# A recurrence and its FFN on one core: a new order for all jobs, and four chunks loaded in runs of 2 KB

## Chip, cores, metric

The kernel runs on one core of a Trainium2 chip. The metric is the device time of one execution, in microseconds (us), the median of several runs. TensorE is called PE here, VectorE DVE, ScalarE ACT, GpSimd POOL, SyncE SP.

## What is computed

A gated linear recurrence along 5824 time steps (4 sequences, 256 channels), then a multiplicative FFN without an activation on all 23296 tokens. Cut to what matters:

```python
a_base = 1.0 / (1.0 + np.exp(-a_param))
log_a = 8.0 * sig_r * np.log(np.clip(a_base, 1e-06, 1.0 - 1e-06))[None, None, :]
a_t = np.exp(log_a)
x_gated = np.sqrt(np.maximum(1.0 - a_t * a_t, 1e-06)) * sig_i * x
for t in range(S):
    h = a_t[:, t] * h + x_gated[:, t]
    y[:, t] = h
...
a = y @ w1
b = y @ w2
out = (a * b @ w3) @ w_out
```

`sig_r` and `sig_i` are the sigmoids of `r_gate` and `i_gate`; w1 and w2 are 256 x 1024, w3 is 1024 x 1024, w_out 1024 x 256.

## The kernel before

The tokens are cut into 47 chunks: chunks 0 and 1 and the last (46) have 256 tokens, the others 512. w3 and w_out are multiplied once at the start (the "fold", `Ft`, `Fc`, `Fm`, `Fe`, eight parts), so that each chunk needs two up projections and one down projection. All products are in bf16.

One chunk passes through these jobs, each a word of the order, with the chunk's number behind it:

- `r`, `i`, `x` (`load`, line 151): three DMAs on SP, 512 KB each. Partition p gets row p of each of four blocks of 128 tokens, in runs of 1 KB. Chunks 0, 2, 3, 4 and 7, which PE turns ("long rows"), have four tokens in a row on a partition instead.
- `R`, `I` (lines 160 to 168): tanh on ACT. `p`, `t` (173, 189, 192): u = (tanh + 1) x, mostly on POOL, the second in two halves.
- `V`, `U` (lines 200, 211): the tanh of r and u are turned, so that channels lie on partitions: by PE into PSUM for a few early chunks, by a transposing DMA on SP for the others (tiles `rt` and `ut`).
- `d` (`decay`, 223): a = exp on ACT, for each half of the channels. `s` (`square`, 231, 233): a squared, on ACT, DVE or POOL, by tables. `q` (`root`, 238): sqrt(1 - a a) on ACT, behind a table load, since exp and tanh share a table that sqrt is not in.
- `g` (`gated`, 248, 251): max and product with the turned u, on DVE, in place. `h` (`scan`, 270): the recurrence, on DVE, two scans a chunk. `y` (`cast`, 280, 282): to bf16, mostly on POOL.
- `a`, `b` (`up`, 299): the up projections on PE in four pairs of 128 columns of w1 and w2; `a` comes in two halves of two matmuls, each with its own PSUM tile, `b` has four matmuls into one PSUM pair. `c` (`copy`, 320 on DVE, 322 on ACT): a half of `a` from PSUM to bf16. `m` (`product`, 337): a times b on DVE, from PSUM.
- `D` (`down`, 357): eight matmuls for 128 tokens. `e` (`evac`, 320, 322): two such results from PSUM. `o` (`store`, 380): to memory, on SP.

`W` (`warm`, 287) are pairs of matmuls on a constant, whose results nobody reads. `L` and `C` load and cast weights.

Every tile comes from a ring of a few buffers (`ring`): among others four PSUM tiles "po" for `a`, `D` and turns, and two PSUM pairs "pb" for `b` and `W`. A tile is taken again when the last reader of its former holder is done, so a matmul can wait for a copy four tiles back, and a `b` for the product of two before. The order of the work is written out by hand in the string `ORDER`, 2449 words, each issued on its engine as it comes; each engine runs its own instructions strictly in that order. Which engine takes a movable job is set by tables ahead of it (`DV_COPY`, `DV_EVAC`, `AC_SQUARE`, `DV_HALF`, `AC_CAST` and others): a copy listed in `DV_COPY`, say, goes to DVE, any other to ACT.

Of the kernel before, what the change touches and what calls it, by code (L numbers as in the profile page):

```python
# [664 lines left out]
```

## Time and profile before

| | |
|---|---|
| time, median of 3 runs | 511.43 us (511.33 to 511.6) |
| span of the profiled execution, first to last instruction | 509.1 us |
| what lies around the span (median less span) | 2.3 us |
| PE busy | 501.7 us, 99%, 3225 matmuls |
| ACT busy | 461.5 us, 91% |
| DVE busy | 431.8 us, 85% |
| POOL busy | 318.0 us, 62% |
| DMA packets on the 16 engines | 85% of the span, 124 MB |

The page gives no time of its own for the profiled execution beside its span. Shares are means over the span: the first 26 us, in which weights arrive, and the last 60, in which the recurrence is over, differ from the middle. "Busy" of PE counts overlapping matmuls, so that it says that PE had work, and not at what rate; durations of single matmuls contain the tail behind the last column.

### The profile page before, as it was taken

The page shows a single profiled execution, that of the slowest core. Times are in us where ns is not written, and L with a number is a line of the kernel's source. Part 1 is how long each engine was busy: PE and PEld are TensorE (multiplying, and loading weights), DVE is VectorE, ACT ScalarE, POOL GpSimd, SP SyncE. Part 2 cuts the span into 40 slices and gives each one's busy share as a digit, 9 for nine tenths or more (in the row PEclk, how much of TensorE's full clock was granted, in tenths as well). Part 3 has the DMA queues.
Part 4 walks back from the last instruction along what each step waited for, and adds up shares of the span by engine and source line. Part 5 has one row for each costly group of instructions (what it writes and reads, how often), then busy time and mean ns, then how long its engine had stood idle before and what let it go on. Part 6 is the DMA issues. An engine that isn't in the chain of part 4 may idle for free.

```text
span 509.1 us, 8891 instructions
## 1 busy us (share of the span) xinstructions
PE 501.7 (99%) x3225; PEld 308.3 (61%) x3225; DVE 431.8 (85%) x417; ACT 461.5 (91%) x708; POOL 318.0 (62%) x269
## 2 busy tenths in 40 slices
PE   7999999999999999999999999999999999999997
PEld 3767665665665656556656556565566655656566
...
GB/s 317 410 411 345 335 316 282 305 286 259 310 220 298 279 285 247 211 302 196 247 305 327 254 286 148 252 243 227 210 246 164 235 298 161 85 166 62 65 51 104
DMA packets 178048, 124.06 MB, mean 244 GB/s; under 512 B 87378, under 2 KB 174036, under 8 KB 178004
## 3 DMA queue, kind: packets, MB, share of 16 engines
...
q8 instruction: 25, 0.41, 0.4%
...
## 4 chain that ended last, share of the span: by engine, by line
PE 92%; ACT 3%; DMA 2%; POOL 1%; DVE 1%; issue 1%; SPq 1%; ACTq 0%; DVEq 0%
PE po L357 30%; PE pb L299 29%; PE pa L299 29%; DMA wf<-in_moe_w_dram 2%; PE pw L436 1%; ACT sa L322 1%; PE ptr L200 1%; PE ptw L425 1%; POOL u_t L192 0%; DVE h_t L270 0%; SPq L151 0%; ACT ot L322 0%; SPq L407 0%; ACT L168 0%; ACT L238 0%
## 5 line engine op out<-in xcount | busy, mean ns | idle before, releaser
L337 DVE TENSOR_TENSOR g_t<-sa,pb 128x1024 bf16<-128x1024 bf16 (+1 forms) x188 | 218.7, 1180 | 58.9 <-PE pb L299 27.6
L299 PEld LDWEIGHTS <-w_sb 128*128 128x128 bf16 x1504 | 146.4, 98 | 144.1 <-issue 1.4
L322 ACT CAST sa<-pa 128x512 bf16<-128x512 f32 (+1 forms) x332 | 179.8, 591 | 27.1 <-PE pa L299 18.9
L299 PE MATMUL pa<-y_t,w_sb 128*128 128x512 bf16 (+1 forms) x752 | 190.2, 372 | 0.2 <-ACT sa L322 0.2
L299 PE MATMUL pb<-y_t,w_sb 128*128 128x512 bf16 (+1 forms) x752 | 184.9, 372 | 0.2 <-ACT w_sb L414 0.2
L357 PE MATMUL po<-wp_sb,g_t 128*128 128x256 bf16 (+1 forms) x1464 | 177.6, 272 | 0.0
L357 PEld LDWEIGHTS <-g_t 128*128 128x128 bf16 x1464 | 142.5, 98 | 39.5 <-issue 0.3
L282 POOL CAST y_t<-h_t 128x1024 bf16<-128x1024 f32 (+2 forms) x47 | 53.8, 1145 | 140.2 <-DVE h_t L270 136.1
L192 POOL TENSOR_TENSOR u_t<-i_t,x_t 128x512 bf16<-128x512 f32 (+1 forms) x90 | 123.3, 1387 | 3.8 <-DMA ut<-u_t 1.8
L270 DVE TENSOR_TENSOR_SCAN h_t<-a_t,h_t,nrm 128x512 f32<-128x512 f32 (+1 forms) x92 | 121.1, 1343 | 1.6
L233 POOL TENSOR_TENSOR nrm<-a_t 128x512 f32<-128x512 f32 x70 | 78.4, 1137 | 7.0 <-ACT a_t L223 4.0
L223 ACT ACTIVATE a_t<-rt,la 128x512 f32<-128x512 bf16 (+1 forms) x82 | 66.1, 823 | 0.0
L322 ACT COPY ot<-po 128x512 f32<-128x512 f32 x84 | 49.1, 589 | 13.2 <-PE po L357 12.9
L173 POOL TENSOR_SCALAR i_t<-i_t 128x1024 f32<-128x1024 f32 (+1 forms) x45 | 55.4, 1233 | 8.3 <-ACT i_t L168 8.3
L251 DVE SCALAR_TENSOR_TENSOR nrm<-nrm,ut 128x1024 f32<-128x1024 f32 (+1 forms) x39 | 53.2, 1365 | 5.2 <-ACT nrm L238 5.2
L168 ACT ACTIVATE i_t<-i_t 128x1024 f32<-128x1024 f32 (+1 forms) x46 | 48.5, 1063 | 0.3 <-DMA i_t<-in_i_gate_dram 0.2
L238 ACT ACTIVATE nrm<-nrm 128x1024 f32<-128x1024 f32 (+1 forms) x47 | 48.4, 1040 | 0.2
L162 ACT ACTIVATE th_r<-r_t 128x1024 bf16<-128x1024 f32 (+1 forms) x41 | 43.5, 1064 | 0.0
L320 DVE CAST sa<-pa 128x512 bf16<-128x512 f32 x36 | 23.5, 684 | 1.4 <-PE pa L299 0.8
L238 ACT ACT_TABLE_LOAD x17 | 21.8, 1283 | 0.4
L287 PE MATMUL warm<-ident 128*128 128x512 bf16 x32 | 10.7, 473 | 1.6 <-DVE ident L441 1.6
L231 ACT ACTIVATE nrm<-a_t 128x512 f32<-128x512 f32 x18 | 11.4, 645 | 0.0
...
## 6 DMA issues: line engine op xcount, KB each, us to landing
...
rt<-th_r SPq DMA_TRANSPOSE x41, 4.7
ut<-u_t SPq DMA_TRANSPOSE x39, 4.4
```

What stands on the lines that cost most here:

```text
L173: (nc.vector if c in DV_PLUS else nc.gpsimd).tensor_scalar(t, t, 1.0, 1.0, op0=ALU.add, op1=ALU.mult)
L192: (nc.vector if (c, half) in DV_HALF else nc.gpsimd).tensor_mul(out=u, in0=t, in1=xt)
L223: nc.scalar.activation(out=a, in_=pr, func=AF.Exp, scale=la4[:, cb:cb + 1], bias=la4[:, cb:cb + 1])
L233: (nc.vector if (c, cb) in DV_SQUARE else nc.gpsimd).tensor_mul(out=n, in0=a, in1=a)
L238: nc.scalar.activation(out=n, in_=n, func=AF.Sqrt, scale=-1.0, bias=1.0)
L251: nc.vector.scalar_tensor_tensor(out=n, in0=n, scalar=1e-3, in1=T["pu", c][:, :, cols], op0=ALU.max, op1=ALU.mult)
L270: nc.vector.tensor_tensor_scan(h[:, cb, :], a[:, cb, :], n[:, cb, :], init, ALU.mult, ALU.add)
L282: (nc.vector if key in DV_CAST else nc.gpsimd).tensor_copy(out=y, in_=h)
L299: nc.tensor.matmul(out=dst, lhsT=w_sb[:, cb, m * P:(m + 1) * P], rhs=T["y", gates_of(c)][:, cb, span(c, mp)], start=(cb == 0), stop=(cb == ...
L322: nc.scalar.copy(out=dst, in_=src_ps)
L337: nc.vector.tensor_mul(out=T["g", z][:, 2 * mp:2 * mp + 2, span(c, mp)], in0=T["sa", c, mp][:, :, :w], in1=T["pb", c, mp][:, :, :w])
L357: nc.tensor.matmul(out=po, lhsT=T["g", c][:, k, j * P:(j + 1) * P], rhs=wp_sb[:, k, cols], start=(k == 0), stop=(k == KD - 1), skip_group_ ...
```

## The change

All 2449 words are the same; up to word 1500 (chunk 27's first up matmul is word 1503) they stand in another order, and the remaining 949 are as before, word for word. The tables have new entries for chunks 0 to 32 where they ended at chunk 16. In all, 34 copies `c` and 4 output copies `e` go from ACT to DVE, 11 squares from POOL to ACT, three halves of u from POOL to DVE, two casts `y` from POOL to ACT; single weight casts and fold steps change engines. PE has the same instructions, and no more and no fewer warm matmuls.

Chunks 38 to 41 are loaded so that a partition gets two tokens in a row (2 KB), twice. Their turned tiles hold the tokens in another order, and decay and gating put them right: in chunks 38 and 39 they read the turned tile in steps of 128 elements, in 40 and 41 they read in a row and write every other float. Gating takes four instructions of 256 elements a chunk instead of one of 1024.

```diff
-    DV_HALF = set()
...
+    DV_HALF = {(9, 1), (16, 0), (30, 1)}
...
+    AC_CAST = {22, 24}
...
+    FOLD_ACT = {('c', 7), ('e', 6), ('e', 7)}
...
+    PAIR_IN = {38, 39}
+    PAIR_OUT = {40, 41}
...
+    def in_pairs(c):
+        return c in PAIR_IN or c in PAIR_OUT
+
+    def split_in(t):
+        return t.rearrange("p (h q j) -> p h q j", h=2, q=P)
+
+    def split_turned(t):
+        return t.rearrange("p (h j q) -> p h j q", h=2, q=P)
...
+        if in_pairs(c):
+            rows = src[nm][starts[c]:starts[c] + width(c), :].rearrange("(h p n) c -> p h n c", h=2, p=P)
+            nc.sync.dma_start(out=T[nm, c].rearrange("p (h n) c -> p h n c", h=2), in_=rows)
+            return
         nc.sync.dma_start(out=T[nm, c][:, :n, cols], in_=rows[:, :, cols])
...
         if long_rows(c):
             a, pr = in_time(a, w // P), turned(pr)
+        elif c in PAIR_IN:
+            a, pr = split_in(a), split_turned(pr).rearrange("p h j q -> p h q j")
+        elif c in PAIR_OUT:
+            a, pr = split_in(a).rearrange("p h q j -> p h j q"), split_turned(pr)
         nc.scalar.activation(out=a, in_=pr, func=AF.Exp, scale=la4[:, cb:cb + 1], bias=la4[:, cb:cb + 1])
...
+        if in_pairs(c):
+            for cb in range(NCB):
+                for hh in range(2):
+                    half = slice(hh * 2 * P, (hh + 1) * 2 * P)
+                    n, u = in_time(T["n", c][:, cb, half], 2), turned(T["pu", c][:, cb, half])
+                    if c in PAIR_OUT:
+                        n, u = n.rearrange("p q j -> p j q"), u.rearrange("p q j -> p j q")
+                    nc.vector.scalar_tensor_tensor(out=n, in0=n, scalar=1e-3, in1=u, op0=ALU.max, op1=ALU.mult)
             return
         n = T["n", c][:, :, cols]
...
-        r0 i0 x0 Lw1.1 Lw1.0 r2 i2 Lw2.0 Lw3.2 x2 E W13 A3. A0. A1. A2. R0.1 R0.0 W3 W10 V0.0 V0.1 I0 t0.1 d0.0 s0.0
-        d0.1 s0.1 q0.0 t0.0 Cw1.1 q0.1 Cw1.0 R2 I2 W5 W8 W0 U0 W4 W11 W6 W12 W7 W9 W2 g0 h0.1 h0.0 y0.1 y0.0 a0.0.1
...
+        r0 E W0 A3. A0. A1. A2. W11 W1 R0.1 V0.1 W7 i0 R0.0 V0.0 I0 x0 W3 t0.0 d0.1 Lw1.1 d0.0 Lw1.0 W4 W15 t0.1
+        Cw1.1 W14 U0 Cw1.0 r2 W12 s0.0 s0.1 q0.0 g0 W10 h0.1 h0.0 W2 i2 Lw2.0 q0.1 W5 g1 W6 y0.1 x2 h1.1 h1.0
...
```

The order at three places. First ACT, from the cast of the first half of w2 to the tanh of chunks 3 and 4. In the order before, `y_t` is chunk 1's, `a_t_249` and `nrm_262` are chunk 2's, `sa` are copies of products of chunks 0 and 1, `r_t_257` and `r_t_364` chunks 3 and 4:

```order
L414 CAST w2_sb_91<-wf_111 128x2x512
L280 CAST y_t_217<-h_t_214 128x256
L223 ACTIVATE a_t_249<-ptr_230,la4_85 128x512 x2
L231 ACTIVATE nrm_262<-a_t_249 128x512 x2
L238 ACT_TABLE_LOAD
L238 ACTIVATE nrm_262<-nrm_262 128x1024
L322 CAST sa_358<-pa_301 128x2x256
L160 ACT_TABLE_LOAD
L160 ACTIVATE th_r_390<-r_t_257 128x1024
L322 CAST sa_399<-pa_350 128x2x256
L322 CAST sa_401<-pa_339 128x2x256
L160 ACTIVATE th_r_431<-r_t_364 128x1024
```

In the new order (`a_t_280` and `nrm_283` are chunk 2's, `r_t_266` and `r_t_270` chunks 3 and 4):

```order
L447 CAST w2_sb_91<-wf_201 128x2x512
L247 ACTIVATE a_t_280<-ptr_228,la4_85 128x512 x2
L255 ACTIVATE nrm_283<-a_t_280 128x512 x2
L262 ACT_TABLE_LOAD
L262 ACTIVATE nrm_283<-nrm_283 128x1024
L355 CAST sa_342<-pa_326 128x2x256
L355 CAST sa_362<-pa_346 128x2x256
L355 CAST sa_369<-pa_364 128x2x256
L180 ACT_TABLE_LOAD
L180 ACTIVATE th_r_379<-r_t_266 128x1024
L180 ACTIVATE th_r_382<-r_t_270 128x1024
L247 ACTIVATE a_t_426<-ptr_416,la4_85 128x512 x2
```

The cast of y is gone from ACT, three copies stand together behind the root, and the two tanh follow one another behind them.

Second POOL, from the first cast of a piece of w3 to chunk 2's y. Before (`i_t_109`, `u_t_322` are chunk 2's, `w3_t` the piece of w3):

```order
L416 CAST w3_t_259<-wf_113 128x1024
L173 TENSOR_SCALAR i_t_109<-i_t_109 128x1024
L192 TENSOR_TENSOR u_t_322<-i_t_109,x_t_115 128x512 x2
L416 CAST w2_sb_91<-wf_251 128x2x512
L416 CAST wo_sb_92<-wf_253 128x1024
L416 CAST wo_sb_92<-wf_255 128x1024
L282 CAST y_t_456<-h_t_387 128x1024
```

In the new order (`i_t_199`, `u_t_324` are chunk 2's; the row of three `y_t` is chunks 0 and 1):

```order
L315 CAST y_t_212<-h_t_193 128x256 x3
L193 TENSOR_SCALAR i_t_199<-i_t_199 128x1024
L212 TENSOR_TENSOR u_t_324<-i_t_199,x_t_214 128x512
L449 CAST w3_t_329<-wf_220 128x1024
L212 TENSOR_TENSOR u_t_324<-i_t_199,x_t_214 128x512
L449 CAST w2_sb_91<-wf_222 128x2x512
L449 CAST wo_sb_92<-wf_224 128x1024
L449 CAST wo_sb_92<-wf_248 128x1024
L315 CAST y_t_428<-h_t_398 128x1024
```

The cast of w3 has moved behind the first half of chunk 2's u.

Third DVE around chunk 23's scan, which the MEMSET marks. Before (`sa<-pa` is a copy, `g_t` a product, `ot<-po` an output copy):

```order
L251 SCALAR_TENSOR_TENSOR nrm<-nrm,ut 128x1024
L265 MEMSET a_t 128x2
L270 SCALAR_TENSOR_TENSOR h_t<-a_t,h_t,nrm 128x512 x2
L337 TENSOR_TENSOR g_t<-sa,pb 128x1024 x2
L251 SCALAR_TENSOR_TENSOR nrm<-nrm,ut 128x1024
L270 SCALAR_TENSOR_TENSOR h_t<-a_t,h_t,nrm 128x512
L337 TENSOR_TENSOR g_t<-sa,pb 128x1024 x2
L270 SCALAR_TENSOR_TENSOR h_t<-a_t,h_t,nrm 128x512
L337 TENSOR_TENSOR g_t<-sa,pb 128x1024 x2
L251 SCALAR_TENSOR_TENSOR nrm<-nrm,ut 128x1024
L337 TENSOR_TENSOR g_t<-sa,pb 128x1024 x2
```

In the new order:

```order
L284 SCALAR_TENSOR_TENSOR nrm<-nrm,ut 128x1024 x2
L298 MEMSET a_t 128x2
L303 SCALAR_TENSOR_TENSOR h_t<-a_t,h_t,nrm 128x512 x2
L284 SCALAR_TENSOR_TENSOR nrm<-nrm,ut 128x1024
L353 COPY ot<-po 128x512
L370 TENSOR_TENSOR g_t<-sa,pb 128x1024 x2
L353 CAST sa<-pa 128x512 x2
L370 TENSOR_TENSOR g_t<-sa,pb 128x1024 x2
L303 SCALAR_TENSOR_TENSOR h_t<-a_t,h_t,nrm 128x512 x2
L370 TENSOR_TENSOR g_t<-sa,pb 128x1024
L303 SCALAR_TENSOR_TENSOR h_t<-a_t,h_t,nrm 128x512
```

Between the products stand copies that ACT had, and the gatings of three chunks with two scans and an output copy follow one another without a product between.

On PE the first turn of chunk 2 (`V2`) now stands ahead of the first up matmuls, where it stood behind four pairs of them; ten warm matmuls lie between the turn of chunk 0's u and `V2`, where fourteen lay between it and the first up matmul.

## Rows read from the trace of the kernel before

**Rows 1.** Stretches: us, length, busy (x) of PE, PEld, DVE, ACT, POOL; PEclk, DMA share, GB/s.
```profile
15.22:26.38 11.16, 10.26 (x101) 8.33 (x102) 10.37 (x17) 11.10 (x16) 8.60 (x9) 1.00 1.04 408
26.38:153.00 126.62, 126.62 (x865) 80.03 (x864) 124.40 (x137) 123.08 (x178) 87.64 (x72) 1.00 1.05 306
153.00:305.00 152.00, 152.00 (x927) 90.51 (x925) 130.14 (x103) 148.69 (x231) 114.10 (x92) 1.00 0.98 270
305.00:400.00 95.00, 94.82 (x582) 56.63 (x580) 78.05 (x65) 89.41 (x139) 61.25 (x50) 1.00 0.83 211
400.00:450.00 50.00, 50.00 (x312) 30.31 (x310) 40.43 (x34) 44.23 (x74) 32.76 (x28) 1.00 0.69 199
```
**Rows 2.** The chain of waits, longest pieces: start us, us, what.
```profile
269.90 2.62 PE po L357 x24
...
278.17 2.16 PE pa L299 x10
...
502.45 3.53 PE po L357 x40
```
**Rows 3.** Timeline of PE from 0 to 9 us: start us, us, instruction, count.
```profile
2.78 1.89 PE L287 MATMUL warm<-ident 128*128 128x512 bf16 x4
...
6.32 2.77 PE L287 MATMUL warm<-ident 128*128 128x512 bf16 x6
```
**Rows 4.** Waits of PE: who waited for whom, us in total, times, longest us.
```profile
PE ptr L200 <- POOL u_t L192: 0.5, 1, 0.5
PE ptw L425 <- POOL w_t L416: 0.4, 1, 0.4
...
PE pa L299 <- ACT sa L322: 0.2, 1, 0.2
```
**Rows 5.** Timeline of PE from 8 to 27.5 us, idle time before in brackets.
```profile
16.47 0.62 PE L425 MATMUL ptw<-ident,w_t 128*128 128x128 bf16 x8 [0.43 <-POOL w_t L416]
...
20.07 0.51 PE L200 MATMUL ptr<-ident,u_t 128*128 128x128 bf16 x6 [0.46 <-POOL u_t L192]
...
26.38 1.02 PE L299 MATMUL pa<-y_t,w_sb 128*128 128x512 bf16 x4
```
**Rows 6.** Timeline of ACT from 7 to 24.5 us.
```profile
14.12 1.04 ACT L414 CAST w_sb<-wf 128x1024 bf16<-128x1024 f32 x1 [0.22 <-DMA wf<-in_moe_w_dram]
15.07 0.40 ACT L280 CAST y_t<-h_t 128x256 bf16<-128x256 f32 x1
15.38 1.44 ACT L223 ACTIVATE a_t<-ptr,la 128x512 f32<-128x512 bf16 x2
...
19.17 1.06 ACT L238 ACTIVATE nrm<-nrm 128x1024 f32<-128x1024 f32 x1
...
20.72 1.28 ACT L160 ACT_TABLE_LOAD   x1
...
22.98 1.05 ACT L322 CAST sa<-pa 128x512 bf16<-128x512 f32 x2
```
**Rows 7.** Timeline of VectorE (DVE) from 7 to 27.5 us.
```profile
14.68 1.28 DVE L320 CAST sa<-pa 128x512 bf16<-128x512 f32 x2
```
**Rows 8.** The gatings (line 251) in two stretches: us, length, busy (x count); then as rows 1.
```profile
26.38:153.00 126.62, 12.29 (x10) 1.00 1.05 306
153.00:305.00 152.00, 18.64 (x13) 1.00 0.98 270
```
**Rows 9.** The scans (line 270) in the same stretches.
```profile
26.38:153.00 126.62, 30.07 (x24) 1.00 1.05 306
153.00:305.00 152.00, 42.80 (x28) 1.00 0.98 270
```
**Rows 10.** Groups of instructions by form: count, busy us, mean ns of one, idle before.
```profile
L223 ACT ACTIVATE a_t<-rt,la 128x512 f32<-128x512 bf16 x80 | 65.0, 828 | 0.0
...
L320 DVE CAST sa<-pa 128x512 bf16<-128x512 f32 x36 | 23.5, 684 | 1.4 <-PE pa L299 0.8
...
L248 DVE SCALAR_TENSOR_TENSOR nrm<-nrm,ptr 128x256 f32<-128x256 f32 x4 | 1.5, 408 | 0.2 <-PE ptr L200 0.2
```

More of the change, by code (lines that the diff above doesn't have):

```diff
@@ new lines @@
+        c16.3.1 c15.3.1 c16.2.1 b15.3 i25 a16.2.0 d22.0 b16.2 a16.3.0 m15.3 c16.3.0 d23.1 x22 D14.1 d22.1 g18
+        d23.0 I22 c16.2.0 D14.0 e14.0 s22.1 h18.0 b16.3 h18.1 a17.0.0 D14.3 c17.0.0 m16.3 r26 p20 t20.1 t20.0
+        x23 D15.1 D14.2 e14.1 m16.2 D15.0 a17.1.0 e15.0 R25 a17.2.1 c17.1.0 c17.2.1 R27 p22 s22.0 t22.0 I25
+        a17.0.1 c17.0.1 I23 U20 b17.0 m17.0 o14.1 a17.2.0 c17.2.0 a17.1.1 c17.1.1 g19 I21 o14.0 R24 a17.3.0
+        b17.2 c17.3.0 m17.2 D16.1 V25 r30 D15.3 D15.2 a17.3.1 b17.1 h19.0 h19.1 D16.0 x21 b17.3 e15.1 c17.3.1
@@ new lines @@
+        R26 y18 a18.0.0 m17.1 o15.0 m17.3 e16.0 a18.1.0 c18.1.0 g20 c18.0.0 s23.0 a18.2.0 a18.1.1 c18.1.1 t22.1
+        i26 c18.2.0 s23.1 a18.0.1 c18.0.1 s21.1 p21 V24 b18.1 d25.0 y19 U22 s25.0 s21.0 d25.1 a18.3.1 I26
+        a19.0.0 m18.1 o16.0 b18.0 m18.0 a18.3.0 h20.0 b18.3 c18.3.1 i24 d24.0 s25.1 c19.0.0 c18.3.0 a18.2.1
+        d24.1 c18.2.1 D16.2 m18.3 b18.2 m18.2 a19.0.1 D16.3 e16.1 a19.1.0 c19.0.1 c19.1.0 x25 x24 V26 a19.1.1
+        c19.1.1 a19.2.0 c19.2.0 b19.0 D17.0 t21.1 m19.0 q23 a19.2.1 t21.0 q22 r28 q21 b19.1 o15.1 D17.1 p23
@@ new lines @@
+        a27.2.1 a27.3.0 D26.0 c27.2.1 c27.3.0 q29 b27.2 m27.1 m27.2 t32.1 o25.0 c27.3.1 U32 V33 q32 D26.1 b27.3
+        a28.0.0 e26.0 c28.0.0 a28.1.0 R36 c28.1.0 D26.2 a28.0.1 c28.0.1 d34.0 i36 g29 h29.0 h29.1 m27.3 y29
+        s34.0 g30 b28.0 D26.3 a28.1.1 D25.2 c28.1.1 d34.1 e26.1 o26.1 V36 o26.0 D25.3 e25.1 b28.1 a28.2.0
+        a28.2.1 c28.2.0 m28.0 m28.1 R37 a29.0.0 c29.0.0 c28.2.1 a29.1.0 b29.0 a29.1.1 h30.0 h30.1 b28.2 t31.0
+        y30 m28.2 I33 c29.1.0 c29.1.1 a29.0.1 D27.0 c29.0.1 a28.3.0 D27.1 d33.0 m29.0 a29.2.1 e27.0 d33.1
@@ new lines @@
+        c32.2.1 d38.1 s36.0 s36.1 s37.0 s35.1 D30.0 y33 b32.2 D30.1 U35 e30.0 s38.0 a33.0.0 s37.1 a33.0.1
+        c33.0.0 c33.0.1 R39 s38.1 a33.2.0 a33.1.0 b32.3 p37 i39 x36 D30.2 q35 g34 m32.2 m32.3 h34.0 b33.0 D30.3
+        V40 c33.1.0 a33.2.1 c33.2.0 c33.2.1 e30.1 h34.1 b33.1 a33.1.1 q36 m33.0 o30.0 r42 c33.1.1 D31.0 I38
+        a33.3.0 V39 i40 D31.1 m33.1 y34 t36.0 t36.1 e31.0 c33.3.0 a33.3.1 b33.2 a34.1.0 r41 b33.3 a34.0.0
+        c34.1.0 c33.3.1 a34.1.1 g35 m33.2 a34.0.1 c34.1.1 h35.0 c34.0.0 d39.0 D32.0 D32.1 b34.0 d40.0 U36 x39
@@ new lines @@
+        c35.3.0 c35.3.1 b35.3 a36.2.0 V41 o32.1 m35.3 t38.0 t38.1 p40 h37.1 y37 p39 q40 e33.1 x40 t39.0 t39.1
+        c36.0.0 c36.2.0 V42 U38 b36.0 a36.2.1 a36.1.1 c36.2.1 D34.0 a36.1.0 c36.1.0 c36.1.1 a36.0.1 c36.0.1
+        D34.1 e34.0 b36.1 o33.1 x41 t40.0 q38 m36.0 m36.1 a36.3.0 d41.0 a36.3.1 a37.0.0 c36.3.0 I41 b36.2 D34.2
+        D34.3 b36.3 e34.1 c36.3.1 t40.1 m36.2 m36.3 p41 o34.0 U39 g38 h38.0 b37.0 R43 x45 i45 a37.1.0 D35.0
+        D35.1 d41.1 c37.0.0 a37.2.0 a37.0.1 c37.1.0 h38.1 a37.1.1 e35.0 D36.0 D36.1 b37.1 c37.2.0 c37.1.1
@@ new lines @@
+        c37.0.1 a37.2.1 d42.0 U40 i43 e36.0 o34.1 o36.0 c37.2.1 m37.0 o35.0 a37.3.0 c37.3.0 b37.2 a37.3.1 y38
+        m37.1 m37.2 a38.1.0 g39 h39.0 h39.1 c37.3.1 a38.0.1 D35.2 b37.3 a38.0.0 I43 D35.3 c38.1.0 c38.0.0
+        c38.0.1 D36.2 D36.3 a38.1.1 g40 e35.1 I42 t41.0 t41.1 y39 b38.0 e36.1 c38.1.1 I45 r45 m37.3 b38.1
+        a38.2.0 a38.2.1 m38.0 a39.0.0 m38.1 c38.2.0 c38.2.1 h40.0 a39.0.1 b38.2 m38.2 d42.1 c39.0.0 c39.0.1
+        a38.3.1 a38.3.0 r46 c38.3.0 c38.3.1 x42 V43 i44 U41 b39.0 a39.2.0 a39.2.1 c39.2.0 c39.2.1 a39.1.1 d43.0
@@ new lines @@
+        c44.1.0 c44.1.1 a45.0.0 a44.2.0 D42.2 c44.2.0 c45.0.0 D42.3 b44.1 a44.2.1 c44.2.1 m44.1 e42.1 a45.0.1
+        b44.2 m44.2 q46 c45.0.1 a44.3.0 a45.1.0 t46.0 b45.0 t46.1 m45.0 U46 g46 a44.3.1 b44.3 D43.0 D43.1
+        c44.3.0 a45.2.0 c45.1.0 c44.3.1 o42.1 a45.3.0 m44.3 c45.2.0 b45.1 e43.0 a45.2.1 a45.1.1 c45.3.0 D43.2
+        D43.3 b45.2 c45.1.1 c45.2.1 h46.0 h46.1 y46 a46.1.0 m45.1 a46.2.0 a45.3.1 o43.0 b45.3 c46.1.0 e43.1
+        c45.3.1 m45.2 a46.0.0 m45.3 c46.2.0 o43.1 a46.0.1 c46.0.0 D44.0 D44.1 a46.2.1 b46.0 D44.2 D44.3 e44.0
@@ L631 @@
+        b46.1 c46.0.1 c46.2.1 a46.1.1 D45.0 D45.1 c46.1.1 m46.0 e44.1 m46.1 b46.2 a46.3.1 a46.3.0 b46.3 D45.2
+        D45.3 e45.0 c46.3.0 c46.3.1 o44.0 o45.0 e45.1 o44.1 o45.1 m46.2 m46.3 D46.0 D46.1 e46.0 e46.1 o46.0
+        o46.1
         """
```

257 lines of the change are left out of this document (114 added, 143 removed), and 10 rows, old and new, of the table DV_COPY.

## Prediction

> **What bounds the kernel now.** I read the table of stretches first [rows 1]. From 26.38 to 450 us TensorE (PE) is busy in all but 0.18 us. A busy PE need not be at its peak, so the next view is the chain of waits, where it runs through the middle and the end of the program [rows 2]: 24 down matmuls take 2.62 us (109 ns each), 10 up matmuls 2.16 us (216 ns each), and no other engine stands in the chain there. That is the upper of the clock's two levels, 2.4 GHz: of the first warm matmuls, six take 0.88 us more than four, 0.44 each, the level of 1.2 GHz [rows 3]. Third, the waits of PE: after 15 us the largest are 0.5 for u of chunk 2 and 0.4 for a cast of w3, and after 26.4 us there is one of 0.2, for a copy on ACT [rows 4].
>
> So the time is PE's work plus a start. The work, from the counts of the kernel's loops: 1408 up matmuls of 512 columns at 216 ns (304.1 us), 96 of 256 columns and 1448 down at 109 (168.3), 16 half-width ones and 160 turns of 128 columns at 56 (9.9; eight turns step through 0.62 us less a tail, [rows 5]), 64 fold matmuls at 109 (7.0): 489.3 us. The 32 warm matmuls are no work. PE's last piece ends at 505.98 us [rows 2], so 16.7 us go to the start; behind it stand 3 us of last copy and store, and 2.3 us outside the profile (median 511.43, span 509.1).
>
> The start has two parts. Until 15.2 us PE cannot have the second up projection: the ACT cast of w2 begins at 14.12 behind a wait for its DMA and takes 1.04 [rows 6]. The change leaves the first eight loads and that cast where they are. From 15.22 to 26.38 (11.16 us, 101 matmuls, [rows 1]) PE does 64 at 109 ns and 32 at 56, that is 8.8 us; the other **2.4 us** are warm matmuls (0.86) and waits. That is nearly all an order can win back.
>
> **The change, part by part.** PE's instructions are the same 3225: a gain can only come from waits.
>
> *The first 26 us.* On ACT a cast of y stood between the cast of w2 and chunk 2's decay, which began at 15.38; it is gone, and the decay can begin where the cast did, at 15.07: 0.31 earlier, and so is the square root, which ended at 19.17 + 1.06 = 20.23 and now ends at 19.92 [rows 6]. The first copy of a product behind it ends at 20.4. It frees one of the four PSUM tiles of the ring "po", for which the up matmuls of chunk 1, pair 3 wait: PE is there at about 19.9, a new wait of 0.6. Four matmuls later (0.44, and 0.2 of tail) the last copy starts at 21.05 (0.5); a table load and the step of a tanh take 2.26 (20.72 to 22.98), the second tanh 1.06 like the root [rows 6]: 24.9. The turn of chunk 4 (0.45) and four matmuls (0.44): 25.8. The other chain goes through VectorE: w2 is cast at 15.16, then PE has 16 matmuls (1.74) and two short waits, 17.4; eight steps of 0.60 on VectorE (two copies take 1.28, [rows 7]) bring 22.2, two scans of 1.2 (the undisturbed mean is 1.25 with its tail, [rows 9]) 24.6, a product and a copy 1.28: 25.9. POOL's cast of y of chunk 2 (1.04) ends before that. So chunk 2's up matmuls start at about 25.93 where it was 26.38 [rows 5]: **-0.45 us**. Gone are PE's waits of 0.43 for w3's cast and of 0.46 for u of chunk 2 [rows 5], since POOL makes half of that u before that cast, and one of two warm pairs; in their place come the 0.6 and about 0.3 ahead of a product's PSUM pair. Bounds: -2.4 (all won) and +0.6 (one more wait like the new one).
>
> *Chunks 2 to 26: copies go from ACT to VectorE.* 34 casts and 4 output copies move. On VectorE each adds 0.60 [rows 7]: +22.8; three halves of u (+1.8) and a few weight steps (-0.6): +24. ACT loses 38 steps of 0.48 (two copies take 1.05, [rows 6]) and gets 11 squares of about 0.5: -12. POOL loses 11 squares, 3 halves and a y: about -17. ACT and POOL gain room. VectorE was busy for 124.4 + 130.1 = 254.5 of 278.6 us between 26.38 and 305 [rows 1]; 24 more make 278.5, full to the brim. Part of that shrinks as it fills: an instruction right behind another overlaps it by 0.08 (two copies 1.28, one 0.68, [rows 7, 10]), which some 90 did not do, 7 us; and the gatings and scans of 153 to 305 us took 18.6 for 13 and 42.8 for 28, against 1.23 and 1.25 each in the stretch before [rows 8, 9], 10.4 us of disturbance. That leaves 261 to 271 us, 94 to 97%. In 26 to 153 us VectorE was 98% and ACT 97% busy [rows 1] without a wait of PE, so I take **0** for new waits; the other bound is +3 (first rival).
>
> *After chunk 27* the order is the same word for word, the tail too: 0. The 0.2 for a copy [rows 4] stays.
>
> *Chunks 38 to 41.* Their 12 loads come in runs of 2 KB, on queues that are 69 to 83% busy [rows 1], for a PE that waits for none of them: 0. Gating such a chunk is four instructions of 256 elements instead of one of 1024: four at 0.41 against one of 1.2 to 1.4 [rows 8, 10], at most +0.4 a chunk. VectorE idles 9.6 us of 400 to 450 and ACT 5.8 [rows 1]: hidden. Of the 16 decays of these chunks half read in steps and half write every other float; no row shows either. The nearest is chunk 0's gating, which writes every fourth float and takes 0.41 for 256 elements, while copies have 0.68 for 512 [rows 10]: a fixed part and no penalty. I take the old 0.83 [rows 10]; double would be 16 x 0.83 = 13 us of ACT at the worst, against 5.6 + 5.8 us idle in the two stretches, so at most +1.5.
>
> The Trainium skill speaks against the reading in steps: its page "SBUF — State Buffer" (section "Door 1: The DMA port swizzle") says that the memory has lines of 16 bytes and that an access which crosses to a new line pays a penalty. No row here reads on-chip memory 256 bytes apart, so the trace neither bears this out nor denies it. By the row the sum is 511.0 us, by the rule 511.2.
>
> **Sum:** 509.1 - 0.45 = 508.65 us of span and 2.33 around it: **511.0 us**, 0.1% under the median. A measurement of this kernel can tell about 0.2% (1.0 us) from no change.
>
> **The rivals.**
> *VectorE becomes the bound (slower).* Between b of chunk 21, pair 2, and b of chunk 22, pair 1, PE has two b of 0.86, five halves of a of 0.43 and six down groups of 0.87 in the new order, 9.1 us; VectorE has two products, three gatings, two scans and an output copy in a row for that time, 8.7 us at undisturbed steps (1.13, 1.15, 1.19, 0.60) and 0.3 until the first can start. A PSUM pair comes back only with its product, so whatever is over goes to PE. Price: if the 10.4 us of disturbance stay, 271 us are wanted of 278, and in-order waits for PE and ACT come on top; VectorE decides from where its idle share falls under 2%, and the 98% of 26 to 153 us would be passed by 1.5 to 3 us: **513 us**. For it: these sums. Against it: 26 to 153 us, as full and without waits, and a POOL with 17 us less work to get in the way. 20%.
>
> *The start wins far more:* the copy that frees the PSUM tile comes when PE needs it, and two thirds of the 2.4 us are won: **509.8 us**. Against it: the root cannot end before 19.9. 10%.
>
> *TensorE's clock falls in the start.* In the new order the first turn of chunk 2 stands ahead of the first up matmuls, and behind the turns of chunk 0 only ten warm matmuls fill the time to it, where fourteen did; PE idles from about 11.7 to 13.2 us. Before, the longest pause after the rise was 0.5 [rows 4]. The granted clock reads 1.00 in all stretches [rows 1], so no row shows a fall. If it fell, the next two groups of 16 up matmuls (1.74 each at 109 ns) would take twice their time at the lower level, as the first warm ones did [rows 3]: +3.5, **514 us**. 4%.
>
> *Steps are dear:* eight decays at twice 0.83 [rows 10] add 6.6 us to ACT under 11.4 idle, and 0.2 are left to PE: **511.2 us**, no difference. 4%. This is the rule of the Trainium skill named above.
>
> *Nothing is won at the start:* the new waits take what the old ones gave: **511.4 us**. 6%.
>
> **How the numbers follow.** The forecast has 56%: 510.2 to 511.5, with 8 of the 56 below 510.4. Faster: 8 + 9 (second rival) = 17%. Slower: 17 (first rival), 4 (clock), 1 (steps) = 22%. The other 61% lie within 0.2%. The range of 510.0 to 513.0 leaves out most of the second rival and the far ends of the first and of the clock, under 2 in 10.
>
> **What would show it.** After: chunk 2's first up matmul at 25.5 to 26.2 us; PE's waits before 26 us led by an ACT copy, not by POOL; VectorE near 455 us busy, ACT near 449, POOL near 300; no PE waits of note from 26 us, PE's last piece near 505.5. The forecast is wrong if PE shows waits for products or copies between 26 and 305 us that sum to over 1 us (first rival), if chunk 2 starts before 25 us (second), if the granted clock leaves 1.00 (third), or if decays of chunks 38 to 41 last over 1.2 us and PE waits behind them.

## The result, and the profile after

The changed kernel takes **513.47 us** (median of 3, 513.11 to 513.86) against 511.43: slower by 2.0 us, a ratio of 1.0041 (95% interval 1.0027 to 1.0056). The forecast of 511.0 and the range of 510.0 to 513.0 missed; the first rival, VectorE as the bound, had been priced at 513. Unaltered on another chip it took 514.31 us (5 executions, 513.31 to 514.97), 1.0059 of the kernel before (1.0046 to 1.0072).

The stretches of the changed kernel, with the columns of [rows 1]:

```profile
15.22:26.38 11.16, 10.08 (x101) 8.08 (x100) 10.91 (x17) 10.90 (x15) 8.42 (x9) 1.00 1.04 408
26.38:153.00 126.62, 125.39 (x844) 79.08 (x857) 124.64 (x138) 122.33 (x174) 84.37 (x73) 1.00 1.06 309
153.00:305.00 152.00, 150.17 (x902) 89.54 (x918) 146.94 (x143) 139.47 (x207) 89.28 (x73) 1.00 0.98 258
305.00:400.00 95.00, 94.24 (x570) 56.44 (x578) 78.11 (x65) 89.56 (x139) 61.39 (x52) 1.00 0.87 225
400.00:450.00 50.00, 49.51 (x313) 31.03 (x318) 40.79 (x46) 44.40 (x73) 32.67 (x27) 1.00 0.66 188
```

From 153 to 305 us VectorE went from 130.14 to 146.94 us busy, 86 to 97%; ACT and POOL came down. PE's busy time lacks 1.83 us there, part of it records of matmuls that are missing from this trace (3172 of 3225), so I took the losses from its waits and from when the same matmul starts in both traces. The waits of PE (who waited for whom, us in total, times, longest), beside [rows 4]:

```profile
PE ptr L220 <- ACT th_r L180: 1.8, 2, 1.4
...
PE pa L332 <- DVE sa L353: 0.7, 2, 0.5
PE pa L332 <- ACT sa L355: 0.7, 2, 0.4
PE pb L332 <- DVE g_t L370: 0.4, 2, 0.2
PE pa L332 <- POOL y_t L315: 0.4, 1, 0.4
```

PE's last matmul starts 2.49 us later than before. Where that arises: nothing in the first 28 us (0.06 us ahead); 0.68 at 53 to 59 us; 0.88 at 236 to 240; 0.12 at 253; 0.60 at 290 to 298; 0.05 at 370; 0.22 at 418. At 118 us 0.13 is lost and at 86 us 0.16 won, where a wait of before is gone. So 2.3 us come from 28 to 305 us, where the forecast had 0. The span grew by 2.5 us and the median by 2.0; what lies around the span came out at 1.9 us instead of 2.3.

What stands behind the largest loss, in the timelines of VectorE and POOL from 231 to 238 us:

```profile
231.46 1.22 DVE L284 SCALAR_TENSOR_TENSOR nrm<-nrm,ut 128x1024 f32<-128x1024 f32 x1
232.78 3.32 DVE L303 TENSOR_TENSOR_SCAN h_t<-a_t,h_t,nrm 128x512 f32<-128x512 f32 x2
236.02 0.66 DVE L353 CAST sa<-pa 128x512 bf16<-128x512 f32 x1
236.79 2.35 DVE L370 TENSOR_TENSOR g_t<-sa,pb 128x1024 bf16<-128x1024 bf16 x2
```

```profile
233.99 1.04 POOL L193 TENSOR_SCALAR i_t<-i_t 128x1024 f32<-128x1024 f32 x1 [2.46 <-ACT i_t L188]
235.11 2.06 POOL L212 TENSOR_TENSOR u_t<-i_t,x_t 128x512 bf16<-128x512 f32 x1
```

and of PE behind them:

```profile
236.74 1.02 PE L332 MATMUL pa<-y_t,w_sb 128*128 128x512 bf16 x4 [0.21 <-DVE sa L353]
...
239.99 0.59 PE L332 MATMUL pa<-y_t,w_sb 128*128 128x512 bf16 x2 [0.49 <-DVE sa L353]
```

Two scans take 2.46 us undisturbed; here 3.32. The second began at 233.98, within 0.01 us of POOL's (tanh + 1), and lasted 2.12 instead of 1.26: it **waited for POOL's instruction to end**. POOL's next one stretches in its turn, 2.06 instead of 1.27. Behind the scans VectorE goes from one instruction to the next, so its copies come later, and PE waits for two of them, at 236.74 and 239.99. The same at 287:

```profile
287.19 2.25 DVE L303 TENSOR_TENSOR_SCAN h_t<-a_t,h_t,nrm 128x512 f32<-128x512 f32 x1
```

```profile
287.09 1.27 POOL L212 TENSOR_TENSOR u_t<-i_t,x_t 128x512 bf16<-128x512 f32 x1
```

The loss at 53 to 59 us has the same origin. A square of chunk 7 on VectorE began 0.04 us behind a product of POOL's and took 1.78 us where the others take 0.68:

```profile
44.31 1.78 DVE L257 TENSOR_TENSOR nrm<-a_t 128x512 f32<-128x512 f32 x1
```

```profile
44.27 2.96 POOL L212 TENSOR_TENSOR u_t<-i_t,x_t 128x512 bf16<-128x512 f32 x2
```

From there VectorE works through without a pause of note to chunk 4's scans, which POOL's cast of y and then PE, at 53.87, wait for.

The rule is the same in all the traces of this case. A scan or gating that starts while POOL runs one of its elementwise instructions lasts longer by what is left of that instruction, less 0.18 us for a scan and 0.135 for a gating (nothing where less than that is left). In the changed kernel's trace: 1.17 us left, 0.99 longer (287.19); 1.16 and 0.98 (301.11); 0.49 and 0.31 (257.57); for gatings 1.02 and 0.89 (321.60), 0.43 and 0.29 (328.42). With 1.26 us for an undisturbed scan and 1.22 for a gating it gives the length of 411 such scans and gatings in the sixteen traces to 0.015 us. The products, which read one operand from PSUM, never stretch: the 176 of 1024 elements last 1.19 to 1.22 us. Nor does a gating that takes u from PSUM: chunk 7's began at 67.52 with 0.71 us of a product of POOL's left, and took 1.21. I call these stretches hold-ups. The Trainium skill has this, on its page "SBUF — State Buffer", section "Who interferes with whom": a VectorE instruction with two inputs in SBUF and a GpSimd instruction that reads SBUF exclude each other, and the one that issues first keeps the ports for its whole length. The trace agrees, to 0.015 us, but for the constant part, of which that section has nothing.

### The profile page after: what moved, and what is told of

Its sections match the earlier page's. It is cut to its first block, busy times and chain, and to the rows that moved or that the text cites. A ratio compares the mean times of both kernels' runs of the same rounds, so it can differ in the third digit from the quotient of the medians.

```text
span 511.6 us, 8876 instructions
## 1 busy us (share of the span) xinstructions
PE 499.4 (98%) x3172; PEld 307.9 (60%) x3225; DVE 451.0 (88%) x470; ACT 453.5 (89%) x681; POOL 294.4 (58%) x255
## 4 chain that ended last, share of the span: by engine, by line
PE 80%; DVE 7%; ACT 5%; issue 3%; DMA 3%; SPq 1%; POOL 0%; DVEq 0%; ACTq 0%
PE po L390 26%; PE pb L332 26%; PE pa L332 24%; DVE g_t L370 3%; DMA wf<-in_moe_w_dram 2%; ACT sa L355 2%; DVE h_t L303 2%; PE pw L469 1%; DMA rt<-th_r 1%; DVE sa L353 1%; PE ptr L220 1%; ACT a_t L247 1%; PE ptw L458 1%; ACT nrm L262 1%; DVE nrm L281 0%
## 5 line engine op out<-in xcount | busy, mean ns | idle before, releaser
L355 ACT CAST sa<-pa 128x512 bf16<-128x512 f32 (+1 forms) x298 | 162.3, 586 | 33.2 <-PE pa L332 21.7
L332 PE MATMUL pa<-y_t,w_sb 128*128 128x512 bf16 (+1 forms) x719 | 185.9, 372 | 2.8 <-DVE sa L353 0.7
L315 POOL CAST y_t<-h_t 128x1024 bf16<-128x1024 f32 (+2 forms) x46 | 49.1, 1069 | 158.6 <-DVE h_t L303 154.9
L212 POOL TENSOR_TENSOR u_t<-i_t,x_t 128x512 bf16<-128x512 f32 (+1 forms) x87 | 119.0, 1383 | 1.8 <-DMA ut<-u_t 0.7
L303 DVE TENSOR_TENSOR_SCAN h_t<-a_t,h_t,nrm 128x512 f32<-128x512 f32 (+1 forms) x92 | 117.4, 1308 | 1.0
L257 POOL TENSOR_TENSOR nrm<-a_t 128x512 f32<-128x512 f32 (+1 forms) x59 | 65.8, 1130 | 20.2 <-ACT a_t L247 13.0
L193 POOL TENSOR_SCALAR i_t<-i_t 128x1024 f32<-128x1024 f32 (+1 forms) x45 | 52.0, 1158 | 8.0 <-ACT i_t L188 8.0
L284 DVE SCALAR_TENSOR_TENSOR nrm<-nrm,ut 128x1024 f32<-128x1024 f32 (+1 forms) x35 | 45.9, 1317 | 3.2 <-ACT nrm L262 2.8
L353 DVE CAST sa<-pa 128x512 bf16<-128x512 f32 x70 | 46.1, 678 | 0.8
L255 ACT ACTIVATE nrm<-a_t 128x512 f32<-128x512 f32 x29 | 18.3, 636 | 0.1
L320 PE MATMUL warm<-ident 128*128 128x512 bf16 x32 | 10.4, 455 | 1.6 <-DVE ident L474 1.6
```

The source lines that it names most:

```text
L193: (nc.vector if c in DV_PLUS else nc.gpsimd).tensor_scalar(t, t, 1.0, 1.0, op0=ALU.add, op1=ALU.mult)
L212: (nc.vector if (c, half) in DV_HALF else nc.gpsimd).tensor_mul(out=u, in0=t, in1=xt)
L257: (nc.vector if (c, cb) in DV_SQUARE else nc.gpsimd).tensor_mul(out=n, in0=a, in1=a)
L303: nc.vector.tensor_tensor_scan(h[:, cb, :], a[:, cb, :], n[:, cb, :], init, ALU.mult, ALU.add)
L315: (nc.vector if key in DV_CAST else nc.gpsimd).tensor_copy(out=y, in_=h)
L332: nc.tensor.matmul(out=dst, lhsT=w_sb[:, cb, m * P:(m + 1) * P], rhs=T["y", gates_of(c)][:, cb, span(c, mp)], start=(cb == 0), stop=(cb == ...
```

## Experiments

**Theory 1:** the losses are hold-ups of VectorE by POOL, and they reach PE because the new order leaves VectorE no room. **Theory 2:** the 2 KB loads carry a share. **Theory 3:** VectorE's own work is too much, whatever POOL does. **Theory 4**, formed after the first four runs: the new start loses time where TensorE's granted clock falls. Each run stands beside executions of the kernel before on its chip, whose medians were 511.12 to 511.34 us.

**The change on chunks 38 to 41 alone, in the kernel before.**

```diff
+    PAIR_IN = {38, 39}
+    PAIR_OUT = {40, 41}
```

> The kernel before with one part of the change alone: chunks 38 to 41 loaded in runs of 2 KB, decays and gatings by halves. Theory 1 (the 2.0 us come from VectorE's instructions that stand behind POOL's in chunks 4 to 29): this part costs nothing, 511.2 to 511.7 us. Theory 2 (the loads and the strided decays carry a share, as the PE wait of 0.33 us at 418 us hints, where it was 0.11): 511.7 to 512.2 us, with the same wait of 0.3 near 416 us. The cast of the first half of w2 on ACT should begin near 14.1 us, as in the profile of before (14.12), if its later start in the changed kernel (14.51) belongs to the new order; near 14.5 if it varies from run to run.

Measured: 511.73 us, ratio 1.0010 (1.0001 to 1.0018). The cast of w2 began at 14.62, in the old order: its time varies between executions. The wait near 416 us is there, 0.33 instead of 0.11. Its cause, in VectorE's timeline of this run, and of the kernel before under it:

```profile
411.03 1.43 DVE L276 SCALAR_TENSOR_TENSOR nrm<-nrm,ut 128x256 f32<-128x256 f32 x4
412.38 2.45 DVE L298 TENSOR_TENSOR_SCAN h_t<-a_t,h_t,nrm 128x512 f32<-128x512 f32 x2
414.75 1.40 DVE L276 SCALAR_TENSOR_TENSOR nrm<-nrm,ut 128x256 f32<-128x256 f32 x4
416.07 2.43 DVE L365 TENSOR_TENSOR g_t<-sa,pb 128x1024 bf16<-128x1024 bf16 x2
```

```profile
410.36 1.22 DVE L251 SCALAR_TENSOR_TENSOR nrm<-nrm,ut 128x1024 f32<-128x1024 f32 x1
...
414.06 1.20 DVE L251 SCALAR_TENSOR_TENSOR nrm<-nrm,ut 128x1024 f32<-128x1024 f32 x1
...
416.60 2.35 DVE L337 TENSOR_TENSOR g_t<-sa,pb 128x1024 bf16<-128x1024 bf16 x2 [0.21 <-PE pb L299]
```

Four short gatings take 1.43 and 1.40 us where one took 1.22 and 1.20: two chunks, 0.41 us more in a row, with 0.21 of idle time ahead of the next product to cover it. The other 0.2 go to PE. Theory 2 holds for 0.3 us (with 0.07 at 368, behind the strided decays).

**The change without that part.**

```diff
-    PAIR_IN = {38, 39}
-    PAIR_OUT = {40, 41}
+    PAIR_IN = set()
+    PAIR_OUT = set()
```

> The changed kernel without the part on chunks 38 to 41. Theory 1: 513.2 to 513.6 us, the PE waits at 53, 236 to 240 and 289 to 298 us all there. Theory 2: 512.7 to 513.1 us. The cast of w2 should begin near 14.5 us again if the new order makes it late.

Measured: 514.94 us (6 executions, 513.14 to 515.96), 1.0063 (1.0045 to 1.0080): slower than either theory allowed; in three of the six executions the mean clock was 0.996 or 0.997. The waits at 53, 236 to 240 and 290 to 298 us are the same, that at 418 is back at 0.11. But PE was 2.8 us behind the kernel before by 30 us: x of chunk 0 landed at 7.61 us, ACT's root waited 1.75 for the squares that stand behind u on VectorE, and PE paused for 2.89. After that the granted clock read 0.91 in 13 to 15 us, 0.50 in 15 to 17 (the lower level, 1.2 GHz) and 0.74 in 17 to 19. The third rival of the prediction does occur, here behind a late load.

**Two words moved**, so that two of the hold-ups do not arise.

```diff
-h22.1 a20.3.1 I24 d26.0 a21.1.0
+h22.1 a20.3.1 d26.0 I24 a21.1.0
...
-d29.1 s29.1 c26.1.0
+d29.1 t30.0 s29.1 c26.1.0
```

> The changed kernel with two words moved, the tables as they are: on ACT a decay of chunk 26 goes ahead of the tanh of chunk 24's input gate, so that POOL's (tanh + 1) of chunk 24 no longer starts as chunk 22's second scan does; on POOL the product of chunk 30's u goes ahead of a square of chunk 29, so that it is over when chunk 27's first scan starts. VectorE has the same instructions in the same order. Theory 1 (a scan that starts while a POOL instruction runs waits for its end, and a full VectorE hands that on to PE): the two scans fall from 2.12 and 2.25 us to about 1.3, and 0.7 to 1.5 us of PE's waits at 236 to 240 and 289 to 298 us go: 512.0 to 512.8 us. Theory 3 (VectorE has too much work of its own, whatever POOL does): 513.3 to 513.7 us.

Measured: 512.99 us (9 executions, 512.20 to 514.64), 1.0031 (1.0021 to 1.0042): below the range of theory 3 and 0.2 above that of theory 1. VectorE and POOL at the first place:

```profile
233.46 2.46 DVE L303 TENSOR_TENSOR_SCAN h_t<-a_t,h_t,nrm 128x512 f32<-128x512 f32 x2
```

```profile
235.37 1.40 POOL L193 TENSOR_SCALAR i_t<-i_t 128x1024 f32<-128x1024 f32 x1 [3.17 <-ACT i_t L188]
```

Both scans run undisturbed, and the 1.5 us at these two places are gone but for 0.03, with not one instruction of VectorE's changed. Theory 3 cannot explain that. But at 134 us a gating now lost by 0.01 us to a product of POOL's:

```profile
133.91 2.38 DVE L284 SCALAR_TENSOR_TENSOR nrm<-nrm,ut 128x1024 f32<-128x1024 f32 x1
```

```profile
133.92 3.49 POOL L212 TENSOR_TENSOR u_t<-i_t,x_t 128x512 bf16<-128x512 f32 x2
```

and 0.6 us were lost there anew, 0.55 at 118 us (0.13 in the changed kernel). In the changed kernel the same gating began at 133.82, 0.06 ahead of the product, and took 1.22. Who wins is decided by hundredths of a microsecond.

**POOL's work left out.**

```diff
+        if 8 <= c < 33:
+            t = t[:, :, :8]
...
+        if 8 <= c < 33 and (c, half) not in DV_HALF:
+            return
```

> The changed kernel in which POOL leaves out most of the gated input of chunks 8 to 32: (tanh + 1) on 8 of 256 columns, no products u (the transposing DMAs read a piece of w1 instead); VectorE, ACT and PE have the same instructions in the same order. Theory 1: the scans and gatings of 153 to 305 us fall to 1.28 and 1.22 us each but for those behind POOL's squares, PE's waits after 60 us fall under 0.5 us in all but for the tail's: 511.7 to 512.3 us. Theory 3: the waits at 236 to 240 and 289 to 298 us stay, 513.0 us or more.

Measured: 511.84 us (1.0009, 1.0000 to 1.0018). The scans of 153 to 305 us, 39.07 us in the changed kernel:

```profile
153.00:305.00 152.00, 35.52 (x28) 1.00 1.02 267
```

PE lost 0.15 us from 150 to 305 us instead of 1.6. VectorE was still 95% busy there. So the hold-ups are needed for the loss. The run also frees the gatings from waiting for POOL's u, but in the changed kernel they waited for it once after 26 us, 0.44 us at 280. The 0.6 at 53 to 59 us (chunks 4 to 7 keep their POOL work) and 0.4 at 118, behind a copy on ACT, remain.

**The changed kernel again.**

> The changed kernel itself, unaltered, on the chip of the runs beside it. If its 513.47 us is what it takes everywhere: 513.1 to 513.9 us. If the start of the new order is open to late loads (in the run without the 2 KB loads the load of x of chunk 0 landed at 7.61 us instead of 6.80, TensorE paused for 2.89 us and its granted clock fell to 0.50 in 15 to 17 us): single runs up to 516 us, and a median above 513.9 us on this chip. Waits of PE at 53 (0.5 us), 236 to 240 (0.9) and 289 to 298 us (0.6) in either case, if they do not hang on a moment's chance; a shift of the start by 0.3 us may move or remove those that do.

Measured: 514.31 us (513.31 to 514.97; one of five executions with a mean clock of 0.997). From 153 us on the losses of the profile stand at the same places to 0.03 us (0.38 and 0.66 at 236 and 239; 0.13, 0.23 and 0.28 at 290 to 297), and so does that of 53; between 110 and 145 us they differ by up to 0.3. Why this chip's other executions take up to 1.7 us more than the profiled one was not found: three have a clock of 1.00 or 0.999 and only one is profiled.

**New order, old copies; old order, new copies.**

```diff
-    DV_COPY = {(0, 0, 0), (0, 1, 0), (1, 0, 0), (1, 1, 0), (1, 2, 0), (2, 0, 0)
...
+    DV_COPY = {(0, 0, 0), (0, 1, 0), (1, 0, 0), (1, 1, 0), (2, 0, 0), (2, 0, 1)
...
```

(for the second run the other way round, and `DV_EVAC` with it)

> The new order with the copies and output copies on the engines of the kernel before (34 copies and 4 output copies go back from VectorE to ACT); all else as in the changed kernel. Theory 1 (a wait needs both a VectorE instruction held up by POOL and a VectorE without room): VectorE falls under 90% in 153 to 305 us, scans held up by POOL stay but PE does not wait for them, and the waits for VectorE in 150 to 305 us sum to under 0.3 us; but ACT, with 38 steps of 0.48 us more in that order and 11 squares beside, would be wanted for 467 us and be full from 153 to 305 us, so that PE waits for ACT's copies: 512 to 516 us. Theory 3 (VectorE's own work is too much): no wait for VectorE, 511.5 to 512.5 us.

> The order of the kernel before with the changed kernel's copies and output copies on VectorE; all else as before. VectorE gets some 25 us more in 153 to 305 us, where it was busy for 130 of 152, and POOL's hold-ups of 10 us there stay, since the order is not made for them. Theory 1: VectorE has no room there and each hold-up goes to PE: 516 to 524 us, VectorE at 98 to 99% in 153 to 305 us. If a full VectorE were harmless: under 513 us.

Measured: 544.52 us and 551.33 us (1.0652 and 1.0789). Both expectations miss by tens of microseconds. In the first PE waits for ACT's copies and for PSUM tiles that ACT empties (three kinds of wait, 8.1, 7.5 and 5.1 us in all); in the second for VectorE's products (10.2) and copies (5.4), with VectorE only 90% busy in 153 to 305 us (136.75 of 152). With engines that run strictly in order, an order and its tables are one object, and the two cannot be priced apart in this way. On theories 1 and 3 these runs decide nothing.

**Every loss undone:** the two moves, the square of chunk 7 from VectorE to ACT, no 2 KB loads.

```diff
-    DV_SQUARE = {(0, 0), (0, 1), (7, 0), (26, 1)}
+    DV_SQUARE = {(0, 0), (0, 1), (26, 1)}
```

> The changed kernel with every loss of the profile undone: the two moves of the run before, the square of chunk 7's first half on ACT instead of VectorE (there it started 0.04 us behind a product of POOL's, took 1.78 us, and PE waited for chunk 4's y at 53 us), and no 2 KB loads. If the account is complete: PE's waits after 26 us fall from 3.8 to under 2 us in all, and with a start as early as before's (cast of w2 at 14.1 to 14.5 us) 510.9 to 511.9 us, no slower than before. If other hold-ups come up as soon as these are gone, as at 134 us in the run with two moves: 512 to 513 us.

Measured: 512.52 us (12 executions, 511.24 to 513.92), 1.0019 (1.0009 to 1.0029). The second branch: the losses at 53, 236, 290 and 418 us are gone, and others came up, 0.4 at 49 and 1.5 from 115 to 149 us, part of it behind the hold-up of 134 us again. In the profiled execution the clock also fell, after a pause of 1.94 us (PE alone, granted clock behind its busy time):

```profile
13.00:15.00 2.00, 1.97 (x14) 0.61 1.04 419
15.00:17.00 2.00, 2.00 (x9) 0.53 1.02 393
```

**The start, guarded; and the start without warm matmuls.**

```diff
-    WARM = [2] * 16
+    WARM = [2, 2, 2, 2, 2, 2, 8, 2, 2, 2, 2, 2, 2, 2, 2, 2]
...
-t0.0 d0.1 Lw1.1 d0.0 Lw1.0 W4 W15 t0.1 Cw1.1 W14 U0 Cw1.0 r2 W12 s0.0 s0.1 q0.0
+t0.0 d0.1 Lw1.1 d0.0 Lw1.0 W4 W15 s0.0 s0.1 t0.1 Cw1.1 W14 U0 Cw1.0 r2 W12 q0.0
```

> The changed kernel with two edits of its start: both squares of chunk 0 go ahead of the second half of its u on VectorE (so that the root on ACT does not wait for the load of x, as it did for 0.16 to 1.75 us in the new order's runs), and the last of the five warm pairs ahead of chunk 2's first turn gets eight matmuls instead of two, which fills PE's pause of 1.4 to 2.9 us there. Theory 4 (a part of the new order's time and most of its spread come from that pause, after which the granted clock falls in some executions): no execution shows a mean clock under 0.999, the spread shrinks to about 1 us, the median falls from 514.3 on such a chip to 513.0 to 513.6 us; what is left over before's 511.3 is PE's later waits (0.6 at 53 to 59, 0.9 at 236 to 240, 0.6 at 289 to 298, 0.3 behind the 2 KB loads). If the start has no part in it: 513.9 us or more.

```diff
-    WARM = [2] * 16
+    WARM = [2, 2, 0, 2, 2, 0, 0, 2, 2, 2, 0, 2, 0, 2, 2, 2]
```

> The changed kernel without the ten warm matmuls ahead of chunk 2's first turn: PE's pause before it grows from 1.4 to 2.9 us to some 3.7 us or more. Theory 4: the granted clock falls to its lower level after the pause in nearly every execution (mean clock 0.996 to 0.997), and the next 3 to 5 us of PE's work take twice their time: 515 to 517 us. If the pause is harmless: as the changed kernel, 513.3 to 514.9 us.

Measured: 514.78 us (6 executions, 513.76 to 516.08) and 515.03 (4, 514.49 to 515.64). Without the ten warm matmuls PE pauses for 4.24 us, the clock falls in all four executions (mean 0.996 to 0.997), and in the profile PE is 1.07 us behind the kernel before by 30 us, where the changed kernel on its second chip was 0.22 ahead: the fall costs some 1.3 us. The stretches of PE there, in this run:

```profile
13.00:15.00 2.00, 1.93 (x12) 0.50 1.05 421
15.00:17.00 2.00, 2.00 (x13) 0.70 1.01 395
```

In the first run, with the pause filled, the clock holds in all six executions, but neither median nor spread came down, as the other branch of its expectation had it: moving the squares delayed the turn of chunk 0's u to 9.99 us (8.46 in the second profile of the changed kernel), behind a pause of 1.95 us. Theory 4 stands for the fall of the clock, and fails for the spread.

**The new start in front of the old order,** plain and guarded.

```diff
-m1.2 b1.3 m1.3 d4.0 Lw3.6 a2.0.1 c2.0.1 s3.1 a2.0.0 c2.0.0
+m1.2 b1.3 m1.3 d4.0 Lw3.6 a2.0.0 a2.0.1 b2.0 a2.1.0 c2.0.1
```

(the seam, behind the 146th word; the words behind it run on the engines that they had before)

> The first 146 words of the new order with their engines (all up to chunk 2's first up matmuls, but for one square of chunk 3), then the kernel before's order and engines for all the rest, no 2 KB loads. Theory 1 (the loss lies behind the start, in an order with no room on VectorE, while the new start itself is a gain of 0.3 to 0.5 us where the loads land as before): PE's waits after 26 us as in the kernel before (1.0 us in all), 510.7 to 511.4 us where the clock holds, and single executions 1 to 3 us longer where it falls. If the new start is what costs: 512 us or more.

> As the run before, with the start guarded: squares of chunk 0 ahead of the second half of its u, and PE's pause filled with warm matmuls. Theories 1 and 4 together: no fall of the clock, PE's waits after 26 us about 1.0 us, 510.5 to 511.1 us, under the kernel before. Otherwise 511.3 us or more.

Measured: 513.85 and 513.66 us (1.0046 and 1.0052). Both miss, by the seam: at 31 us PE waits 2.46 us for POOL's cast of a piece of w3, which the new start loads later than the old order wants it, and 1.2 us there in the guarded run. From 35 us to the end PE loses another 0.22 and 0.02 us, so the old body has no loss of its own in either. By 28 us, ahead of the seam, PE was 0.4 us behind the kernel before in the plain run, whose cast of w2 began at 14.94, and 1.2 behind in the guarded one. The guard did not keep the clock in every execution: in two of six its mean was 0.997.

**More room on VectorE, the rest alike.**

```diff
+        if 8 <= c < 33:
+            cols = slice(0, P)
+            n = T["n", c][:, :, cols]
```

> The changed kernel in which the gatings of chunks 8 to 32 work on 256 of their 1024 elements (0.41 us instead of 1.22, some 20 us less for VectorE over 60 to 305 us); POOL, ACT and PE have the same instructions in the same order. Theory 1 (a hold-up reaches PE only where VectorE has no room): VectorE falls to about 90% in 153 to 305 us, hold-ups of over 2 us in all remain there, yet PE's waits for VectorE from 150 to 305 us fall from 1.5 us to under 0.4: 512.0 to 513.2 us where the changed kernel takes 513.5 to 514.3. If hold-ups reach PE whatever room there is: waits of over 1 us remain there.

Measured: 512.92 us (12 executions, 511.50 to 515.71), 1.0036 (1.0022 to 1.0051).

```profile
153.00:305.00 152.00, 150.70 (x909) 90.49 (x925) 136.28 (x143) 140.10 (x209) 85.86 (x74) 1.00 0.99 260
```

VectorE is 90% busy there, 3.3 us of hold-ups remain (one of 1.00 us at 286.80, at the place that cost PE 0.6), and PE's loss from 150 to 305 us is 0.52 instead of 1.63, of which 0.4 is a wait for an output copy on ACT. So room is needed too: theory 1 in both halves. Five of the twelve executions had a mean clock of 0.993 to 0.997 and took 513.4 to 515.7 us.

**The kernel before again.**

> The kernel before, unaltered, for a second profile of it. If the start of the new order is no slower by itself and the times of landing vary from run to run: the cast of w2 on ACT begins somewhere between 13.9 and 14.9 us (14.12 in the first profile), and PE's waits after 26 us are the same eight small ones, 1.0 to 1.1 us in all, with VectorE's hold-ups in 153 to 305 us near 10.6 us again.

Measured: 511.23 us, one execution. The cast of w2 began at 14.45 and PE was 0.35 us behind the first profile by 28 us and 0.36 at the end; the hold-ups in 153 to 305 us are the same.

## Why the prediction was wrong

- **The step that failed** is the one on chunks 2 to 26: "I take 0 for new waits". The new waits were 2.3 us, 0.68 of them at 53 to 59 and 1.6 from 153 to 305 us. It had the numbers (94 to 97% of VectorE's time, 10.4 us of "disturbance") but treated the disturbance as a load, to be added up, and not as what it is: single stops of up to 1.1 us, set off where POOL has begun an instruction first, if only by hundredths of a microsecond. The new order did bring it down, to 4.1 us: 39.07 us for 28 scans less 28 x 1.25, and 17.21 for 14 gatings, just 14 x 1.23. Before, 10.4 us cost PE nothing, with VectorE idle for 21.9 of 152 us; after, 4.1 us cost 1.6, with 5.1 idle. The amounts of work were right: VectorE 451.0 us busy (455 forecast), ACT 453.5 (449), POOL 294.4 (300).
- **The comparison with 26 to 153 us** misled. VectorE is 98% full there without a wait of PE in the kernel before, but its scans and gatings are at their shortest there [rows 8, 9]: two hold-ups, 0.20 us at 69 and 0.12 at 118. In these runs fullness with few hold-ups cost little, hold-ups with room cost little, and together they cost; the run with POOL's work left out (0.15 us lost) and the run with more room on VectorE (0.52, 0.4 of it an ACT copy) show one half each.
- **The first rival** was right in its price (513) and its engine, but not in its place: the row of two products, three gatings and two scans after chunk 21 cost PE 0.12 us, at 253. Its rule, "the 10.4 us of disturbance stay", did not come true.
- **The start:** -0.45 was forecast, -0.06 was found in the profile. The new waits came as worked out: 0.59 for the copy that frees a PSUM tile (0.6 forecast), 0.38 ahead of a product's PSUM pair (0.3). What failed is "the change leaves the first eight loads and that cast where they are": they stand where they stood, but the cast of w2 began at 14.51 instead of 14.12, and chunk 2's up matmuls at 26.32, which is the forecast 25.93 and those 0.39. In two profiles of the kernel before, 14.12 and 14.45, the whole program moves by 0.35. With the cast at 14.18 (the two words moved) chunk 2's up matmuls began at 25.98, 0.40 us ahead. Measured from the cast, the forecast gain is there: those matmuls begin 11.80 to 11.83 us behind it in five profiles of the new start (both of the changed kernel, two words moved, POOL's work left out, new start in front of the old order) and 12.26 to 12.30 in three of the old one. Left out are profiles in which the clock fell, the cast did not wait for its load, the start was guarded or the copies were others. The work of the start was judged rightly; the landing of the load was taken as fixed.
- **Chunks 38 to 41:** "hidden" was wrong by 0.3 us. The 9.6 us that VectorE idles from 400 to 450 us are not where the two gatings stand; 0.21 was. The strided decays cost little: there are 8, not 16 as I wrote; reading in steps took 0.87 to 0.92 us, writing every other float 0.86 to 0.91, the plain ones 0.83. By the Trainium skill ("SBUF — State Buffer", "Door 1: The DMA port swizzle") the steps should cost; the trace puts it at a tenth at most, on ACT. PE waits for 0.05 of it: chunk 38's second decay took 0.89 us where it took 0.83 before, ACT has no pause from there to the copy that PE waits for at 370, and that wait is 0.39 to 0.42 us in the runs with these loads, 0.34 or 0.35 in those without (the two runs with order and copies of different kernels left aside).
- **The clock** held in the profile of the changed kernel (granted 1.00 after a pause of 1.41 us), as forecast with 96%, but the rival is real: in the new order's variants it fell after pauses of 1.94, 2.89 and 4.24 us and held after one of 1.95 and two of 2.09. A mean clock of 0.997 or less stands in 11 of the 57 executions with the new order's start unaltered (the changed kernel and the runs that change only what lies behind its start, without those of other copies), and in 1 of 72 of the kernel before beside them; 4% was too little. Its price is 1.3 us by the run without warm matmuls, 1.6 by the profile with every loss undone (chunk 2's up matmuls 13.43 us behind the cast), not 3.5.

No version was faster than the kernel before. The best new-order variant that does all the work, with every loss undone, is 0.2% slower than it. The start holds 0.4 to 0.5 us to be won where the clock holds, which a measurement of this kernel cannot tell from no change, and 1.3 us or more to be lost where it falls.

What stays open: the spread of the new order's executions with a full clock (513.8 to 516.1 us with the guarded start), which the single profiled execution of each run does not show.
